# The 48 short logits products of a routed part in two portions of 24, and the scatters of one-unit blocks released one by one

## The chip, the cores and the metric

The kernel runs on one core of one Trainium2 chip. The metric is the device time of one execution in microseconds, as the median of several runs; lower is better. One further execution was taken by the hardware profiler, and all views below come from it.

## The reference

The input is x, 8 sequences of 3584 tokens of 192 floats. Stage one is a causal depthwise convolution of 7 taps, whose taps are a softmax over 7 weights for each of 8 heads (24 channels a head). Stage two is a mixture of experts with one expert for each token:

```
logits = x @ w_gate                       # 8 experts
local  = sigmoid(x @ w_local)
e[s]   = argmax(logits[s])   if s == 0 or local[s] < 0.5   else e[s-1]
out[s] = softmax(logits[s])[e] * (relu(x[s] @ w1[e]) @ w2[e])     # 192 -> 1024 -> 192
```

All of it is float32. There are 28672 tokens in all.

## The kernel before, in words

The tokens are worked on in 16 **parts** of 1792 tokens. For each part VectorE and ScalarE compute the convolution (`conv`, lines L378 and L388), and then the part is **routed** (`route`): its logits are computed, the expert of each token is found by a long chain of small VectorE operations, and each token's row is scattered into a table of slots in DRAM (`put`, L777), sorted by expert. Parts 0 and 1 are handled by a special path at the start (`wide`, `wide_route`); the other 14 go through `route`.

A **unit** is 128 slots of one expert. A **block** is one unit (n = 1) or two units (n = 2) of one expert. The 142 blocks are the main work. The first 35 blocks or so have one unit, the bulk after about 267 us has two, and the last 20 have one again. For block i, SyncE's queue loads the expert's weights (`load_w`, L906, 1.5 MB, four buffers) and the rows (`load_rows`, L913) three blocks ahead. TensorE then does, in this order:

- `hidden` of block i (L963): products with w1 in two groups, `two` = 0 and 1. After each group ScalarE applies the ReLU (L968). The PSUM tiles come from `hps_p`, which has four buffers.
- `turn` of block i + 1 (L360): transposes of the next rows into the PSUM tile of `xps_p`, which has one buffer; ScalarE copies them out (L947, L949).
- `output` of block i (L980): products with w2 into `yps_p`. ScalarE and VectorE scale and add the two halves (L988, L992), and GpSimd scatters the rows to the output (L996).

Float32 products show as two weight loads and two matmuls each in the trace. "A pair" below is one LDWEIGHTS with its MATMUL, so 48 products are 96 pairs. One-unit blocks hold 48 pairs of L963, 8 of L360 and 32 of L980; two-unit blocks hold 48, 16 and 64.

Between these steps, `step(time)` is called three times a block: after `turn`, inside `output` (`step(1.2)`, after L988 is issued) and after `output`. It takes VectorE operations from two generators, `route` and `conv`, until their estimated times add up to `time`. When `route` yields "hop", the rest of this `step` goes to `conv`, and `route` goes on in the next `step`. The order of all instructions is fixed when the program is built; nothing is decided at run time.

The logits of a part (`logits`) are where the change lies. VectorE transposes the rows into the tile z (L572). Then TensorE runs 48 short products (L582): 64 rows by 32 columns of weights, 128 columns of data, in two halves of the rows and four groups of columns, so eight of them can be in the array at a time. They accumulate over six steps b in two PSUM tiles of `hps_p`. ScalarE copies the results out (L587), and VectorE transposes and sorts them (L590, L598). So each of the 14 parts has one unbroken run of 96 short pairs at L582, put into TensorE's order where `route` happens to reach it: in ten parts between L360 and L980 of a two-unit block, in one between L360 and L980 of a one-unit block, and in three after L980 (in one-unit blocks).

Two scatters of rows (`put`) go with each block that has any to do; they are held back until a ReLU is done. `put(relu)` adds that wait to the scatter on GpSimd's queue. In two-unit blocks one is released by the ReLUs of `two` = 0 and one by those of `two` = 1; in one-unit blocks both are released by those of `two` = 1.

Of the kernel before, what the change touches and what calls it, by code (L numbers as in the profile page):

```python
# [8 lines left out]
F32 = mybir.dt.float32  # L9
# [8 lines left out]
P = 128  # L18
# [19 lines left out]
BT = 2 * UT  # L38
KT = BT // P
# [24 lines left out]
Q = 32  # L64
DQ = D // Q
TQ = (NT + 3) // 4
# [15 lines left out]
def kernel(  # L82
# [10 lines left out]
    nc = tc.nc  # L93
# [11 lines left out]
    xps_p = ctx.enter_context(tc.tile_pool(name="xps_p", bufs=1, space=PSUM))  # L105
    hps_p = ctx.enter_context(tc.tile_pool(name="hps_p", bufs=4, space=PSUM))
# [77 lines left out]
    wgb, wgq = wg[:, :3, :], wg[:, 3:, :]  # L184
# [5 lines left out]
    def z_tile():  # L190
        return yt.tile([P, 3 * NH * TB + NB * DR], F32, name="z")
# [119 lines left out]
    rows = cst.tile([Q, 2, Q], F32, name="rows")  # L311
# [42 lines left out]
    def halves():  # L354
        return [(half, slice(half * DR, (half + 1) * DR)) for half in range(2)]
# [210 lines left out]
    def logits(g, y_sb):  # L566

        nc.gpsimd.tensor_copy(y_sb[:, :, Y0 + D:IX], y_sb[:, :, Y0 + P:Y0 + D])  # L568
        z = z_tile()[:, :NT * D].rearrange("p (t d) -> p t d", d=D)
        for t in range(0, NT, TQ):  # L570
            u = min(t + TQ, NT)
            nc.vector.transpose(z[:, t:u, :], y_sb[:, t:u, Y0:Y0 + D])  # L572
            yield 0.2 * (u - t)
        yield "hop"


        lps = [hps_p.tile([P, TQ * Q], F32, name="hps") for half in range(2)]
        begin = [min(TQ * j, NT - TQ) for j in range(4)]
        for b in range(DQ):
            for j in range(4):  # L580
                for half, rows in halves():
                    nc.tensor.matmul(lps[half][Q * j:Q * j + Q, :], lhsT=wgq[rows, b, :],  # L582
                                     rhs=z[rows, begin[j]:begin[j] + TQ, b * Q:(b + 1) * Q],
                                     start=(b == 0), stop=(b == DQ - 1))
        ls = sm.tile([P, 2, TQ * Q], F32, name="ls", bufs=1)
        for half in range(2):
            nc.scalar.copy(ls[:, half, :], lps[half])  # L587
        yield "hop"
        lq = sm.tile([P, 2 * TQ, Q], F32, name="lq", bufs=1)
        nc.vector.transpose(lq.rearrange("p t e -> p (t e)"), ls.rearrange("p h x -> p (h x)"))  # L590
        yield 0.4
        lt = sm.tile([P, NT + 2, E + 1], F32, name="lt")
        for r in range(4):
            for j in range(4):
                t, u = TQ * j, min(TQ * (j + 1), NT)
                at = r // 2 * TQ + t - begin[j]
                e0 = r % 2 * (E + 1)
                nc.vector.tensor_copy(lt[Q * r:Q * r + Q, t:u, :],  # L598
                                      lq[Q * j:Q * j + Q, at:at + u - t, e0:e0 + E + 1])
                yield 0.12  # L600
        return lt
# [168 lines left out]
    def put(behind=None):  # L770


        if not to_put:
            return
        g, rows, to = to_put.pop(0)
        nc.gpsimd.nop()
        ins = nc.gpsimd.indirect_dma_start(  # L777
            out=slots[:, :], in_=rows, in_offset=None,
            out_offset=bass.IndirectOffsetOnAxis(ap=to, axis=0)).ins
        if behind is not None:  # L780
            tc.add_manual_dep(ins, behind.ins.name, SYNC, reason="scatters apart")
        if puts:
            tc.declare_no_dep(ins, group="puts", reason="slots of their own")
        if g:
            tc.declare_no_dep(ins, group="gets", reason="those slots were full before")
        puts.append((g, ins))
        tc.add_to_no_dep_group("puts", ins)
        tc.add_to_no_dep_group(f"puts{g}", ins)
# [163 lines left out]
    def hidden(n, wb, xT, shares=(1, 1)):  # L952
        hT = hp.tile([P, FK, BT], F32, name="hT")
        w = slice(0, n * P)


        for two in range(2):
            hps = [hps_p.tile([P, 2, BT], F32, name="hps") for half in range(2)]
            for d in range(KD):
                for j in range(2):  # L960
                    f0 = (d * 4 + two * 2 + j) * P
                    for half, rows in halves():
                        nc.tensor.matmul(hps[half][:, j, w], lhsT=wb[rows, f0:f0 + P],  # L963
                                         rhs=xT[rows, d, w], start=(d == 0 and j == 0),
                                         stop=(d == KD - 1), skip_group_check=True)
            for half in range(2):
                m = half * 4 + two * 2
                relu = nc.scalar.activation(hT[:, m:m + 2, w], hps[half][:, :, w], Act.Relu)  # L968
            for _ in range(shares[two] if n == KT else (0, sum(shares))[two]):
                put(relu)  # L970
        return hT

    def output(n, wb, xg, hT):

        yps = [yps_p.tile([P, 512], F32, name="yps") for half in range(2)]
        for m4 in ([0, 1, 4, 5], [2, 3, 6, 7]):
            for k in range(n):
                for m in m4:
                    for half, rows in halves():
                        nc.tensor.matmul(yps[half][:, k * D:(k + 1) * D],  # L980
                                         lhsT=hT[rows, m, k * P:(k + 1) * P],
                                         rhs=wb[rows, WA + m * D:WA + (m + 1) * D],
                                         start=(m == 0 and k == 0), stop=(m == FK - 1),
                                         skip_group_check=True)
        o_sb = op.tile([P, KT, D], F32, name="o_sb")
        y = [[yps[half][:, k * D:(k + 1) * D] for half in range(2)] for k in range(n)]
        for k in range(n):
            nc.scalar.activation(o_sb[:, k, :], y[k][0], Act.Copy, scale=xg[:, k, 0:1])  # L988

        step(1.2)  # L990
        for k in range(n):
            nc.vector.scalar_tensor_tensor(o_sb[:, k, :], y[k][1], xg[:, k, 0:1], o_sb[:, k, :],  # L992
                                           Alu.mult, Alu.add)

            nc.gpsimd.nop()
            sent = nc.gpsimd.indirect_dma_start(  # L996
                out=out, in_=o_sb[:, k, :], in_offset=None,
                out_offset=bass.IndirectOffsetOnAxis(ap=xg.bitcast(I32)[:, k, IX:], axis=0),
                bounds_check=N - 1, oob_is_err=False)
            tc.declare_no_dep(sent.ins, group="sent", reason="each token has one slot")  # L1000
            tc.add_to_no_dep_group("sent", sent.ins)
# [1 line left out]

    LEAD = 2
    LATE = 3
    st = {"block": 0, "conv": 1, "cgen": None, "route": 1, "rgen": None, "routed": 1}

    def start_conv():
        g = st["conv"] + 1
# [14 lines left out]
    def start_route():  # L1024
        done = st["conv"] - (st["cgen"] is not None)
        if st["rgen"] is None and st["route"] < done:
            st["route"] += 1
            st["rgen"] = route(st["route"])

    def route_op():  # L1030
        c = next(st["rgen"], None)
        if c is None:
            st["rgen"] = None
            st["routed"] = st["route"]
        return c

    def step(time):

        start_route()
        start_conv()  # L1040
        go = st["rgen"] is not None
        while time > 0:
            c = route_op() if go else conv_op()
            if c is None:
                if not go:
                    break
                go = False
            elif c == "hop":
                go = False
            elif c == "placed":  # L1050
                pass
            else:
                time -= c
# [76 lines left out]
    xT, _ = turn(blocks[0][1], xgs[0])  # L1130
# [8 lines left out]
    for i, (_, n, _, _) in enumerate(blocks):  # L1139
        st["block"] = i  # L1140
        ensure(i)
        weights(i + AHEAD)
        if i == LATE:
            x_in[3] = load_x(3)
        hT = hidden(n, wbs[i], xT, (1, 1) if i else (0, 0))
        if i + 1 < len(blocks):
            xT, copied = turn(blocks[i + 1][1], xgs[i + 1])
            if len(to_put) > NT // 2 and n == KT:
                put(copied)
        step(2.1 if n == 1 else 4.2)  # L1150
        output(n, wbs.pop(i), xgs.pop(i), hT)
        step(1.3 if n == 1 else 3.0)

    kind, _, at, group = spare[0]
    any_left = nc.values_load(tabi[kind, group][at:at + 1, 0:1], min_val=0, max_val=DUMMY,  # L1155
                              skip_runtime_bounds_check_because="an entry of the table")
    with tc.If(any_left < DUMMY):
        for block in spare:
            blocks.append(block)
            i = len(blocks) - 1  # L1160
            n = block[1]
            xg = load_rows(i)
            wb = load_w(i)
            xT, _ = turn(n, xg)
# [68 lines left out]
```

## Time and profile before

| what | value |
|---|---|
| median of 7 runs | 1337.73 us (1335.65 to 1341.74) |
| the profiled execution | 1335.88 us, span 1334.2 us |
| TensorE matmuls, weight loads busy | 98%, 95% of the span |
| VectorE, ScalarE, GpSimd busy | 58%, 44%, 37% |
| granted TensorE clock, mean | 0.998 |
| DMA busy, 60 to 335 us / 335 to 935 us | 0.91 / 0.67 |
| L980, L963, L360, L582 matmuls busy | 643.7, 636.4, 62.0, 26.4 us |

A busy share of TensorE says only that some matmul was in flight. Matmuls overlap, so what a run of them costs is read from when the next line begins, and an interval in which too few were in flight can hide in a busy time. The table of waits names what ended an engine's idle time; "issue" stands for idle time in which the profile shows nothing that the engine waited for.

### The profile page before, as it was taken

Reading aid. Unit: us, or ns where it says so; the run is one execution under the profiler, and the core shown is the slowest. Engines: PE = TensorE matmul, PEld = TensorE weight load, DVE = VectorE, ACT = ScalarE, POOL = GpSimd, SP = SyncE. Lnnn points to the kernel's source line nnn. Section 1 sums busy time; section 2 is a strip of 40 time slices with the busy share of each in tenths; the row PEclk is TensorE's granted clock in tenths of the full one; section 3 lists DMA queues with packets and bytes.
Section 4 is the critical chain, followed back from the end, with each engine's and each line's share of the span. In section 5 each row is a group of like instructions: output and inputs, shape, how many; then the busy total and the mean of one; then the engine's idle time right before and its main releaser. Section 6 shows DMA issues by size and latency. Waiting matters only on the chain. (4 is left out here: it accounts for less than half of the span.)

```text
span 1334.2 us, 41246 instructions
## 1 busy us (share of the span) xinstructions
PE 1309.5 (98%) x16682; PEld 1267.8 (95%) x16682; DVE 779.1 (58%) x2434; ACT 583.1 (44%) x1431; POOL 492.5 (37%) x538
## 2 busy tenths in 40 slices
PE   8799999999999999999999999999999999999997
PEld 7799999999999999999999999999999999999997
DVE  6879897877878787878777878786610000000000
ACT  5345554544444444444444444444343333334443
POOL 4445343534243434343434343434344211211111
PEclk9999999999999999999999999999999999999999
DMA  5899999967575757575757575756566555556893
GB/s 187 279 354 390 388 371 357 385 244 276 197 281 197 294 202 291 199 282 202 289 195 287 202 293 205 289 206 230 204 235 223 201 185 188 194 195 230 320 332 126
DMA packets 67297, 340.35 MB, mean 255 GB/s; under 512 B 12576, under 2 KB 23191, under 8 KB 47650
## 3 DMA queue, kind: packets, MB, share of 16 engines
q1 hardware_dynamic: 44784, 284.88, 59.4%
q0 software_dynamic: 22320, 52.82, 10.5%
q8 instruction: 133, 2.18, 0.6%
q14 instruction: 58, 0.48, 0.1%
q10 hardware_dynamic: 2, 0.00, 0.0%
HBM read 284.73 MB, written 53.41 MB: 253 GB/s over the span
## 5 line engine op out<-in xcount | busy, mean ns | idle before, releaser
L980 PE MATMUL yps<-wb,hT 64*128 64x192 f32 x7328 | 643.7, 326 | 5.5 <-DVE o_sb L992 2.8
L963 PE MATMUL hps<-xT,wb 64*128 64x256 f32 (+1 forms) x6816 | 636.4, 336 | 3.8 <-issue 2.4
L980 PEld LDWEIGHTS yps<-wb,hT 64*128 64x128 f32 x7328 | 605.5, 188 | 11.6 <-issue 6.6
L963 PEld LDWEIGHTS hps<-xT,wb 64*128 64x128 f32 x6816 | 592.0, 187 | 25.0 <-issue 4.3
L996 POOL DMA_INDIRECT out_dram<-o_sb,xg x229 | 232.2, 1014 | 602.4 <-DVE o_sb L992 540.7
L968 ACT ACTIVATE hT<-hps 128x512 f32<-128x512 f32 (+1 forms) x568 | 261.5, 512 | 371.8 <-PE hps L963 284.3
L388 DVE SCALAR_TENSOR_TENSOR y_sb<-x_sb,c,y_sb 128x336 f32<-128x336 f32 x672 | 377.2, 571 | 18.6 <-issue 0.5
L992 DVE SCALAR_TENSOR_TENSOR o_sb<-yps,xg,o_sb 128x192 f32<-128x192 f32 x229 | 87.5, 414 | 472.9 <-ACT o_sb L988 459.2
L777 POOL DMA_INDIRECT slots<-y_sb,posi x228 | 228.0, 1000 | 210.6 <-ACT hT L968 90.5
L988 ACT ACTIVATE o_sb<-yps,xg 128x192 f32<-128x192 f32 x229 | 86.8, 418 | 323.9 <-PE yps L980 321.4
L949 ACT COPY xT<-xps 64x256 f32<-64x256 f32 (+1 forms) x284 | 92.2, 325 | 6.9
L947 ACT COPY xT<-xps 128x512 f32<-128x512 f32 (+1 forms) x142 | 72.5, 511 | 4.5 <-issue 1.9
L360 PEld LDWEIGHTS xps<-ident,xg 64*128 64x128 f32 x916 | 61.9, 138 | 5.2 <-issue 0.4
L378 ACT ACTIVATE y_sb<-x_sb,c 128x336 f32<-128x336 f32 x112 | 63.7, 581 | 1.0
L360 PE MATMUL xps<-ident,xg 64*128 64x64 f32 x916 | 62.0, 221 | 0.0
L572 DVE STREAM_TRANSPOSE z<-y_sb 128x768 f32<-128x768 f32 (+1 forms) x56 | 45.4, 852 | 0.4
L598 DVE COPY lt<-lq 32x36 f32<-32x36 f32 x224 | 40.8, 182 | 3.5
L582 PE MATMUL hps<-z,wg 64*32 64x128 f32 x1344 | 26.4, 273 | 2.7 <-issue 2.7
L582 PEld LDWEIGHTS hps<-z,wg 64*32 64x32 f32 x1344 | 19.9, 105 | 6.9 <-issue 6.1
L590 DVE STREAM_TRANSPOSE lq<-ls 128x256 f32<-128x256 f32 x14 | 6.2, 440 | 13.5 <-ACT ls L587 13.5
L568 POOL COPY y_sb<-y_sb 128x896 f32<-128x896 f32 x14 | 13.3, 952 | 0.0
L556 PE MATMUL yps<-y_sb 112*128 112x194 f32 x64 | 11.5, 331 | 1.8 <-DVE y_sb L550 1.8
(240 smaller groups left out, 384.0 us busy)
## 6 DMA issues: line engine op xcount, KB each, us to landing
wb<-in_w_dram SPq DMA_DIRECT2D x138, 1536.0 KB
x_sb<-in_x_dram SPq DMA_DIRECT2D x14, 1920.0 KB
xg<-slots SPq DMA_DIRECT2D x87, 259.0 KB
xg<-slots SPq DMA_DIRECT2D x53, 129.5 KB
wb<-in_w_dram SPq DMA_DIRECT2D x12, 512.0 KB
out_dram<-o_sb,xg POOLq DMA_INDIRECT x229
slots<-y_sb,posi POOLq DMA_INDIRECT x228
x_sb<-in_xb_dram SPq DMA_DIRECT2D x4, 768.0 KB
```

Of the source, the lines that this page charges most:

```text
L360: nc.tensor.transpose(to, src[rows], identity=ident[rows, rows])
L378: nc.scalar.activation(cols(h), chans(h, 0), Act.Copy, scale=c[:, h, 0:1])
L388: nc.vector.scalar_tensor_tensor(cols(h), chans(h, k), c[:, h, k:k + 1], cols(h), Alu.mult, Alu.add)
L777: ins = nc.gpsimd.indirect_dma_start(out=slots[:, :], in_=rows, in_offset=None, out_offset=bass.IndirectOffsetOnAxis(ap=to, axis=0)).ins
L947: nc.scalar.copy(first, by)
L949: copied = nc.scalar.copy(to[rows, :, 2], at[(DR, 0)[half]:(P, DR)[half], :, 0])
L963: nc.tensor.matmul(hps[half][:, j, w], lhsT=wb[rows, f0:f0 + P], rhs=xT[rows, d, w], start=(d == 0 and j == 0), stop=(d == KD - 1), skip_g ...
L968: relu = nc.scalar.activation(hT[:, m:m + 2, w], hps[half][:, :, w], Act.Relu)
L980: nc.tensor.matmul(yps[half][:, k * D:(k + 1) * D], lhsT=hT[rows, m, k * P:(k + 1) * P], rhs=wb[rows, WA + m * D:WA + (m + 1) * D], start= ...
L988: nc.scalar.activation(o_sb[:, k, :], y[k][0], Act.Copy, scale=xg[:, k, 0:1])
L992: nc.vector.scalar_tensor_tensor(o_sb[:, k, :], y[k][1], xg[:, k, 0:1], o_sb[:, k, :], Alu.mult, Alu.add)
L996: sent = nc.gpsimd.indirect_dma_start(out=out, in_=o_sb[:, k, :], in_offset=None, out_offset=bass.IndirectOffsetOnAxis(ap=xg.bitcast(I32)[ ...
```

## The change

The 48 short products of a part are cut at b = 3 into two portions of 24 (48 pairs each), and longer products run between the two.

- Where `route` reaches the products in the `step` between `turn` and `output` (`st["ahead"]`), the first portion is put there, and `route` then hops. The second portion and ScalarE's copies come in the next `step`, inside `output`: between L980 of this block and L963 of the next. The PSUM tiles are from `hps_p` as before, and are held longer. Eleven parts go this way.
- Where `route` reaches them elsewhere, the first portion is put there, into the tile of `xps_p`, and the second one is left as a function in `st["amid"]`. `hidden` of the next block calls it after its first group (`two` = 0): between 12 products of L963 and the 12 that follow. Three parts go this way, the first, second and fourth of the 14.
- The rule that in one-unit blocks both scatters wait for the second pair of ReLUs is gone; they are released one by one, as in two-unit blocks.

No product, copy or scatter is added or taken away. In the order of instructions the portions are the only thing that moves on TensorE. On VectorE the transposes and copies after the logits (L590, L598) come a few operations of `conv` later, behind the L992 of the block. On SyncE's queue one load of a part's input moves behind one load of rows and one of weights, and on GpSimd's queue two scatters move ahead of one copy (L568).

```diff
-        lps = [hps_p.tile([P, TQ * Q], F32, name="hps") for half in range(2)]
+        if st["ahead"]:
+            lps = [hps_p.tile([P, 2 * BT], F32, name="hps") for half in range(2)]
+        else:
+            both = xps_p.tile([P, 2, 512], F32, name="xps")
+            lps = [both[:, half, :] for half in range(2)]
+        lps = [a[:, :TQ * Q] for a in lps]
         begin = [min(TQ * j, NT - TQ) for j in range(4)]
-        for b in range(DQ):
-            for j in range(4):
-                for half, rows in halves():
-                    nc.tensor.matmul(lps[half][Q * j:Q * j + Q, :], lhsT=wgq[rows, b, :],
-                                     rhs=z[rows, begin[j]:begin[j] + TQ, b * Q:(b + 1) * Q],
-                                     start=(b == 0), stop=(b == DQ - 1))
+        def products(bs):
+            for b in bs:
+                for j in range(4):
+                    for half, rows in halves():
+                        nc.tensor.matmul(lps[half][Q * j:Q * j + Q, :], lhsT=wgq[rows, b, :],
+                                         rhs=z[rows, begin[j]:begin[j] + TQ, b * Q:(b + 1) * Q],
+                                         start=(b == 0), stop=(b == DQ - 1))
         ls = sm.tile([P, 2, TQ * Q], F32, name="ls", bufs=1)
-        for half in range(2):
-            nc.scalar.copy(ls[:, half, :], lps[half])
-        yield "hop"
+        def others():
+            products(range(DQ // 2, DQ))
+            for half in range(2):
+                nc.scalar.copy(ls[:, half, :], lps[half])
+        products(range(DQ // 2))
+        if st["ahead"]:
+            yield "hop"
+            others()
+            yield "hop"
+        else:
+            st["amid"] = others
+            while st["amid"]:
+                yield "hop"
...
-            for _ in range(shares[two] if n == KT else (0, sum(shares))[two]):
+            for _ in range(shares[two]):
                 put(relu)
+            if st["amid"]:
+                st["amid"]()
+                st["amid"] = None
...
+        st["ahead"] = True
         step(2.1 if n == 1 else 4.2)
+        st["ahead"] = False
```

## The prediction

> **What bounds the kernel now.** I read the page first, then TensorE's table of waits, then the timeline of TensorE around the logits of each part. The page says that TensorE's matmuls are in flight for 98% of the span at a granted clock of 0.998, and of L582, the line that is changed:
>
> ```profile
> L582 PE MATMUL hps<-z,wg 64*32 64x128 f32 x1344 | 26.4, 273 | 2.7 <-issue 2.7
> ```
>
> Its 1344 matmuls are 14 parts by 96 pairs, and they cover 26.4 us. The change leaves their number alone, so only their neighbourhood can pay. The waits of the weight loads, first from 60 to 275 us (one-unit blocks), then from 275 to 1330 us:
>
> ```profile
> PEld hps L582 <- issue: 6.1, 14, 0.6
> PEld hps L963 <- issue: 4.3, 13, 0.5
> ```
>
> ```profile
> PEld yps L980 <- issue: 4.8, 16, 0.9
> ```
>
> No wait for a DMA stands among them: weights and rows are there in time. What TensorE waits for is "issue", that is, its own instructions. The timeline of TensorE shows a clean case, the last part, in a two-unit block, and the block after it:
>
> ```profile
> 927.74 5.35 PE L963 MATMUL hps<-xT,wb 64*128 64x256 f32 x48
> 932.92 0.41 PE L360 MATMUL xps<-ident,xg 64*128 64x64 f32 x8
> 933.26 1.59 PE L582 MATMUL hps<-z,wg 64*32 64x128 f32 x96
> 934.79 5.47 PE L980 MATMUL yps<-wb,hT 64*128 64x192 f32 x64
> 940.09 5.35 PE L963 MATMUL hps<-xT,wb 64*128 64x256 f32 x48
> ...
> 950.77 4.49 PE L963 MATMUL hps<-xT,wb 64*128 64x256 f32 x40
> ```
>
> From the first L963 to the next, the block with logits takes 940.09 - 927.74 = 12.35 us, the one without 950.77 - 940.09 = 10.68: a clean stage costs 1.67 us. The 96 pairs start 13.9 ns apart ((1.59 - 0.27) / 95, where 0.27 is one matmul), together 1.32 us. The other 0.35 us are entering and leaving: the short products start only when the matmul before has nearly ended, and the same holds when they leave.
>
> Two of the early parts look different (the third of the 14, then the first):
>
> ```profile
> 205.91 1.29 PE L582 MATMUL hps<-z,wg 64*32 64x128 f32 x56
> 207.42 0.42 PE L582 MATMUL hps<-z,wg 64*32 64x128 f32 x5 [0.22 <-issue]
> ...
> 209.69 0.67 PE L582 MATMUL hps<-z,wg 64*32 64x128 f32 x23 [0.33 <-issue]
> 210.29 2.87 PE L980 MATMUL yps<-wb,hT 64*128 64x192 f32 x32
> ```
>
> ```profile
> 88.83 1.23 PE L582 MATMUL hps<-z,wg 64*32 64x128 f32 x38
> 90.36 0.42 PE L582 MATMUL hps<-z,wg 64*32 64x128 f32 x4 [0.31 <-issue]
> ...
> 91.80 1.08 PE L582 MATMUL hps<-z,wg 64*32 64x128 f32 x52 [0.35 <-issue]
> 92.81 1.39 PE L963 MATMUL hps<-xT,wb 64*128 64x128 f32 x20
> ```
>
> Some pairs run at full speed, then TensorE gets a handful of instructions every 0.75 us, then the rest come in a burst. I read this as a store of ready instructions that the short pairs (14 ns each, against 83 to 107 ns for the long ones in two-unit blocks) empty faster than it is filled. The supply is slower here, in the stretch where DMA is 0.91 busy (0.67 later).
>
> **The pool that can be won.** Stage times by the timeline, from the first L582 to the next line: 3.98, 2.20, 4.38, 2.33 us for the first four parts, 1.53 for a clean one. The four lose 2.45 + 0.67 + 2.85 + 0.80 = 6.8 us. The other ten run through L582 without a gap, but some of their L980 stall afterwards: their blocks take 13.06, 12.53, 12.66, 12.96, 12.62, 13.45, 12.53, 12.48, 12.35, 12.35 us, 3.5 us over ten clean ones. Blocks without logits of the same stretch lie within 1.4 us of 10.68 in sum, so the 3.5 belong to the stages.
>
> **The change part by part.**
>
> *More entries and exits (certain, on the path).* Each part gets one more run of short pairs. Between L980 and L963 the timeline's starts are 0.25 us into the run and 0.20 out of it, and the direct turn from L980 to L963 that this replaces is 0.15: 0.30 us net. For the three portions amid L963 no such entry is in the trace; after L360 (matmul 221 ns) it takes 0.15, after L980 (326 ns) 0.25, so after L963 (273 or 376 ns) 0.20 to 0.30, less its own step of 0.10 to 0.20, plus 0.20 out: 0.30 again. Bounds 0.20 and 0.45. 14 x 0.30 = +4.2 us (2.8 to 6.3).
>
> *Two-unit blocks (ten of the parts).* Half the run empties half as much of the store, and 64 pairs of L980 at 83 ns (5.3 us) lie between the portions. At its emptiest the store gave 96 short pairs and 26 long ones (part at 668.9 us, then a stall of 0.65 us). With 48 short pairs fewer it lasts 48 x 83 ns = 4 us longer, beyond that stall. I take -3.3 of the 3.5 us (-1.5 to -3.5).
>
> *Third part (one-unit block, "ahead").* It runs 56 pairs before its first real stall, so 48 pass untouched. Then 32 pairs of L980 need 2.7 us, in which the supply gave only 17 pairs before, and some 8 are left: about 7 pairs short, one stall of 0.6. -2.85 + 0.6 = -2.2 us (0 to -2.85).
>
> *First, second and fourth part (portion two amid L963).* Portion one stands exactly where the whole run stood, and their stalls come after 33 to 44, 28 and 33 pairs, all inside the first 48. They stay. What is saved is at most a tail, -0.3 in all; what may be added is a stall before portion two, because 24 pairs of L963 at 58 ns do not refill the store: +0.6 once. Together +0.3 us (-2.5 to +1.8, the upper end being a stall of 0.6 in each of the three).
>
> *Copies and tiles.* ScalarE's two L587 (0.27 us each) move behind L988 or between the ReLUs. The tile of `xps_p` is wanted by `turn` only after 24 more pairs of L963 (1.4 us), which hides them; without that cover 0.5 us in each of three blocks. The `hps_p` tiles held longer are wanted by `two` = 1 of the next block, 1.4 to 2.6 us later. 0. VectorE's L590 and L598 come later by two to four `conv` operations of 0.57 us; L992 moves ahead of them, and scatters of the part keep their place in GpSimd's order. VectorE's longest waits are for ScalarE, not the reverse. 0.
>
> *SyncE.* One load of x (1.9 MB) goes behind one load of rows and one of weights, one block (5.5 us) later; it is needed after half a part of convolution (24 operations of 0.57 us = 14 us). 0.
>
> *Earlier release of scatters.* GpSimd in the block at 86 us:
>
> ```profile
> 87.59 0.96 POOL L777 DMA_INDIRECT slots<-y_sb,posi  x1 [1.66 <-issue]
> 88.86 0.94 POOL L777 DMA_INDIRECT slots<-y_sb,posi  x1 [0.31 <-issue]
> 90.11 0.99 POOL L996 DMA_INDIRECT out_dram<-o_sb,xg  x1 [0.30 <-DVE o_sb L992]
> ```
>
> The first of the three would go some 1.4 us earlier, in idle time. Behind it on GpSimd are the second scatter and L996; L996 waits for L992, which ended at 89.80, as did the second scatter, so it gains nearly nothing. TensorE waits for none of these. 0 (-1 to +1, since a DMA moved against the short pairs could change their supply).
>
> *Sum.* +4.2 - 3.3 - 2.2 + 0.3 = -1.0 us. The profiled execution of 1335.88 (span 1334.2 and 1.7 around it) becomes 1334.9; it lay 1.85 below the median shown, so the median becomes 1336.7. That is 0.07% less: no change. I count 0.2% (2.7 us) as about what a measurement of this kernel can tell.
>
> A rule weighed. The row: in the clean parts 96 short pairs, 192 instructions, run without a gap, and the early parts stop after 28 to 56 pairs. The Trainium skill, "TensorE: Matmul & The Clock Gate", the table at its head, gives TensorE a queue 64 deep. That would be 32 pairs, near the three early stops, and it speaks against this change, for a portion of 48 pairs overruns it too: by the rule alone every portion would stall, 28 x 0.6 us, +16.8 + 4.2 - 10.3 = some +11 us (an estimate). The clean parts contradict that, so my sum goes by the rows.
>
> **The rivals.** *Stalls go almost wholly* (faster). If a stall is set off by the length of a run and not by how full the store was, all portions pass: -6.8 - 3.5 + 4.2 = -6.1, 1331.6 us. For it: after one stall, parts two and four run 63 to 68 pairs in one burst. Against: their first stall comes by pair 33. Chance 0.29 with all that gains over 2.7 us.
>
> *The supply sets the pace in one-unit blocks* (slower). Then a portion amid L963 or after L980 finds the store empty, and the stalls only move. For it: L963 shows issue stalls there without any logits (4.3 us). Price: +4.2, the early parts win nothing and two or three new stalls of 0.6 come, the later parts win only 1.5: +4.2 + 1.5 - 1.5 = +4.2, 1341.9 us. It decides if portion two of the early parts begins with fewer than 48 pairs in store. Chance 0.27 with all that loses over 2.7 us.
>
> *The split does nothing and the scatters decide*: the portions' gain and loss cancel, and the release shifts times by up to 1 us: within the 0.2%.
>
> **How the numbers follow.** The middle case has 0.44 (the last rival included): faster 0.29, same 0.44, slower 0.27. The range runs to the middle of each neighbouring case and somewhat beyond: 1332.3 to 1341.3 us.
>
> **What would show it.** Right: two-unit blocks with logits all at 10.68 + 1.67 + 0.30 = 12.65 us; the third part without repeated gaps in its first portion; the first, second and fourth with a gap still near pair 30; two more starts of 0.2 to 0.25 us for each part. Wrong: gaps at L963 or L980 after second portions in the early blocks, waits of L360 for the `xps_p` tile, or early blocks that got shorter by 2 us each.

## The result, and the profile after

| | before | changed |
|---|---|---|
| median on the chip of the first measurement | 1336.81 us (1333.37 to 1341.74, 34 runs) | 1339.48 us (1339.04 to 1342.71, 13 runs) |
| ratio, 95% interval | | 1.0027 [1.0018, 1.0036] |
| the profiled execution, and its span | 1335.88 us, 1334.2 us | 1339.83 us, 1338.1 us |
| same on two chips of the experiments (3 and 15), medians | 1320.62 us (25 runs), 1319.99 us (25 runs) | 1322.33 us, 1322.3 us |
| ratios there | | 1.0014 [1.0004, 1.0024], 1.0015 [1.0006, 1.0025] |

The changed kernel is a little slower: by 0.27% by the ratio and 0.20% by the medians, about as much as the prediction thought could be told at all. All experiments ran on three chips (numbers 3, 9 and 15 on record) on which the very same kernel takes some 17 us less. I call these the 1320-us chips, and that of the first measurement the 1337-us chip. The record has no number for the latter, so that the 17 us belong to the chip itself, and not to its condition at that time, is the likely reading and not shown. Nearly everything below hangs on that difference.

In the changed kernel the lines are: hidden products L985 (before L963), logits L591 (L582), output products L1005 (L980), ReLU L990 (L968), scaling L1013 (L988), scatter of slots L799 (L777), scatter of outputs L1021 (L996).

**The two-unit blocks.** TensorE's timeline at the last part, 1337-us chip, the columns being start, length, engine, line, operation and count:

```profile
931.51 5.35 PE L985 MATMUL hps<-xT,wb 64*128 64x256 f32 x48
936.69 0.41 PE L360 MATMUL xps<-ident,xg 64*128 64x64 f32 x8
937.03 0.94 PE L591 MATMUL hps<-z,wg 64*32 64x128 f32 x48
937.90 5.47 PE L1005 MATMUL yps<-wb,hT 64*128 64x192 f32 x64
943.30 0.94 PE L591 MATMUL hps<-z,wg 64*32 64x128 f32 x48
944.17 5.45 PE L985 MATMUL hps<-xT,wb 64*128 64x256 f32 x48
...
954.95 1.25 PE L985 MATMUL hps<-xT,wb 64*128 64x256 f32 x10
```

The block takes 944.17 - 931.51 = 12.66 us (12.65 was forecast). The one after it takes 954.95 - 944.17 = 10.78 instead of 10.68, and its hidden products 5.45 instead of 5.35: 0.10 us that the forecast did not have. Eight of the ten blocks are at 12.66, two at 12.78 and 12.83; no portion there has a gap.

**The parts in one-unit blocks.** The third part, which had paused again and again:

```profile
209.86 0.89 PE L591 MATMUL hps<-z,wg 64*32 64x128 f32 x18
211.03 0.80 PE L591 MATMUL hps<-z,wg 64*32 64x128 f32 x30 [0.29 <-issue]
211.76 2.87 PE L1005 MATMUL yps<-wb,hT 64*128 64x192 f32 x32
214.56 0.94 PE L591 MATMUL hps<-z,wg 64*32 64x128 f32 x48
```

One gap after 18 pairs, the rest unbroken. The first part has one of 0.15 us after pair 29 of its first portion, the second part one of 0.31 us after pair 42 of its second portion, the fourth none; nothing like the former trickle is left.

**The waits, 60 to 275 us.** TensorE's weight loads by what they waited for (total us, times, longest):

```profile
PEld yps L1005 <- ACT hT L990: 14.0, 21, 1.0
PEld hps L985 <- issue: 2.8, 11, 0.4
...
PEld xps L591 <- issue: 1.8, 5, 0.6
PEld hps L591 <- issue: 1.1, 3, 0.6
```

The issue waits at the logits fell from 6.1 to 2.9 us. But output products now wait 21 times for the ReLUs, nearly always in ordinary one-unit blocks without logits. In the same table of before this line was

```profile
PEld yps L980 <- ACT hT L968: 0.7, 2, 0.4
```

Here is one such wait, the block that starts at 182.89, on three engines (TensorE, ScalarE, GpSimd):

```profile
182.89 2.84 PE L985 MATMUL hps<-xT,wb 64*128 64x128 f32 x48
...
185.68 1.52 PE L1005 MATMUL yps<-wb,hT 64*128 64x192 f32 x16
187.48 1.57 PE L1005 MATMUL yps<-wb,hT 64*128 64x192 f32 x16 [0.27 <-ACT hT L990]
188.88 0.50 PE L985 MATMUL hps<-xT,wb 64*128 64x128 f32 x6
```

```profile
184.48 0.66 ACT L990 ACTIVATE hT<-hps 128x256 f32<-128x256 f32 x2 [0.51 <-ACT y_sb L378]
187.04 0.66 ACT L990 ACTIVATE hT<-hps 128x256 f32<-128x256 f32 x2 [1.90 <-PE xps L360]
```

```profile
184.23 1.06 POOL L1021 DMA_INDIRECT out_dram<-o_sb,xg  x1 [1.30 <-DVE o_sb L1017]
185.60 0.97 POOL L799 DMA_INDIRECT slots<-y_sb,posi  x1 [0.30 <-issue]
```

The second group of L985 is done at 185.73 (182.89 + 2.84). Its ReLUs start at 187.04, 1.3 us later, though ScalarE is idle (the row names L360, which TensorE had done by then as well; the tile that the ReLUs read is L985's). Ahead of both lies the start of the scatter that the change released earlier, at 185.60, 1.44 us before the ReLUs. The output products that read these ReLUs start late, and the block takes 188.88 - 182.89 = 5.99 us instead of 5.45. In the kernel before, a block at nearly the same time shows the same delay in a small dose: a scatter starts at 182.95, TensorE's second group ends at 183.56 by the same timeline, and the ReLUs start 1.39 us after the scatter did.

```profile
184.34 0.66 ACT L968 ACTIVATE hT<-hps 128x256 f32<-128x256 f32 x2 [0.93 <-PE xps L360]
```

```profile
182.95 1.06 POOL L996 DMA_INDIRECT out_dram<-o_sb,xg  x1 [0.92 <-DVE o_sb L992]
```

There the ReLUs were 0.8 us late, and the block lost 0.07 us. So there is a slack of some 0.74 us, and the change pushed the delay beyond it.

**The ledger.** Times from the first hidden product of a block to the next, summed over blocks, in the two profiled executions of the 1337-us chip, beside the terms of the forecast:

| stretch | before, us | changed, us | difference | forecast |
|---|---|---|---|---|
| the four parts in one-unit blocks and the block behind (8 blocks) | 65.54 | 61.49 | -4.05 | 1.2 - 2.2 + 0.3 = -0.7 |
| ten two-unit blocks with a part | 126.99 | 126.90 | -0.09 | 3.0 - 3.3 = -0.3 |
| the ten blocks behind them | 107.00 | 107.83 | +0.83 | 0 |
| the other 26 one-unit blocks up to 267 us (269 us) | 146.85 | 156.04 | +9.18 | 0 |
| to the end of the first two blocks | 65.37 | 63.60 | -1.76 | 0 |

The first four lines add to +5.9. The last line is no part of the change that I can name: on the 1320-us chips the same point lies between 63.2 and 65.2 us in the fifteen profiled executions, whichever variant runs. The executions as a whole differ by +3.95 us, the medians by +2.67.

Of the 26 blocks of the fourth line, four have no scatter to release (they start at 159.6, 165.0, 221.0 and 226.4 us in the changed kernel). These four take 5.45 us each; the other 22 take 5.84 to 6.46. That ties the longer blocks to the scatters and not to the split, which no block of this line contains.

**Signals after a scatter.** The trace holds the moment at which a semaphore, the signal from one engine to another, moves. I compared it with the end of the matmul that moves it, and sorted by whether the matmul ended within 1.4 us after GpSimd started an indirect DMA. "Late" is more than 0.3 us; the usual delay is 0.01 us. TensorE's signals:

| execution | 92 to 260 us: late, within 1.4 us | late, otherwise | 330 to 900 us: late, within 1.4 us | otherwise |
|---|---|---|---|---|
| before, 1337-us chip | 88 of 127 | 1 of 75 | 57 of 236 | 0 of 143 |
| changed, 1337-us chip | 81 of 147 | 0 of 48 | 33 of 249 | 0 of 129 |
| before, a 1320-us chip (f2) | 1 of 128 | 0 of 81 | 7 of 267 | 0 of 111 |
| changed, a 1320-us chip (f1) | 1 of 122 | 0 of 85 | 0 of 257 | 0 of 125 |

On the 1337-us chip more than half of TensorE's signals sent in the 1.4 us after such a start come late in the one-unit blocks. In the changed kernel the late ones arrive 1.49 us (median) after the scatter's start, as if held until then. On the other chip this hardly happens. ScalarE's starts agree. I took the second ReLUs of the one-unit blocks from 63 to 270 us for which ScalarE had been idle. Where the products ended within 1.4 us of a scatter's start, the ReLUs began over 0.3 us late in 10 of 24 cases before and 23 of 29 after the change on the 1337-us chip, in 0 of 22 and 0 of 27 on the other; where they did not, never.

For the signals of ScalarE and VectorE the trace shows no such thing. On the 1337-us chip it lacks the moments of 240 of ScalarE's 1428 signals and 295 of VectorE's 1764 in the kernel before (53 of TensorE's 1088; in f2 it lacks 2, 8 and none), and where one is missing, the next one of that engine would pass for a late one. The receiver can be looked at instead. Here, 0.49 us after the scatter that started at 88.86 us, ScalarE ends at 89.35 and VectorE starts 0.03 us later, though the trace has no signal of ScalarE in the next 3.8 us:

```profile
88.93 0.42 ACT L988 ACTIVATE o_sb<-yps,xg 128x192 f32<-128x192 f32 x1 [1.29 <-PE yps L980]
```

```profile
89.38 0.42 DVE L992 SCALAR_TENSOR_TENSOR o_sb<-yps,xg,o_sb 128x192 f32<-128x192 f32 x1 [2.60 <-PE yps L980]
```

In the two profiled executions of that chip I found six such cases with VectorE idle; it started 0.03 us after ScalarE's end in four, 0.18 and 0.35 us after it in two.

The Trainium skill, "Perfetto Trace Analysis", Per-engine timelines, lists the spreading of a semaphore update as a step behind a matmul's recorded end and gives no time for it. The trace has 0.01 us for it mostly, and 1.3 us in these blocks.

### The profile page after: what moved, and what is told of

Same layout as the page of the kernel before. It is cut to its first block, busy times and chain, and to the rows that moved or that the text cites. A ratio compares the mean times of both kernels' runs of the same rounds, so it can differ in the third digit from the quotient of the medians.

```text
span 1338.1 us, 41275 instructions
## 1 busy us (share of the span) xinstructions
PE 1311.1 (98%) x16682; PEld 1242.6 (93%) x16682; DVE 781.3 (58%) x2434; ACT 582.9 (44%) x1431; POOL 491.0 (37%) x538
## 5 line engine op out<-in xcount | busy, mean ns | idle before, releaser
L1005 PE MATMUL yps<-wb,hT 64*128 64x192 f32 x7328 | 637.2, 326 | 12.6 <-ACT hT L990 8.4
L985 PE MATMUL hps<-xT,wb 64*128 64x256 f32 (+1 forms) x6816 | 627.4, 336 | 0.7 <-issue 0.7
L1005 PEld LDWEIGHTS yps<-wb,hT 64*128 64x128 f32 x7328 | 595.1, 187 | 22.8 <-ACT hT L990 15.3
L985 PEld LDWEIGHTS hps<-xT,wb 64*128 64x128 f32 x6816 | 564.6, 187 | 41.0 <-issue 2.8
L1021 POOL DMA_INDIRECT out_dram<-o_sb,xg x229 | 232.1, 1014 | 598.7 <-DVE o_sb L1017 534.0
L990 ACT ACTIVATE hT<-hps 128x512 f32<-128x512 f32 (+1 forms) x568 | 261.7, 512 | 403.1 <-PE hps L985 253.5
L799 POOL DMA_INDIRECT slots<-y_sb,posi x228 | 226.7, 994 | 219.8 <-ACT hT L990 84.3
L1013 ACT ACTIVATE o_sb<-yps,xg 128x192 f32<-128x192 f32 x229 | 86.8, 418 | 308.8 <-PE yps L1005 303.1
L360 PEld LDWEIGHTS xps<-ident,xg 64*128 64x128 f32 x916 | 52.2, 139 | 7.4
L360 PE MATMUL xps<-ident,xg 64*128 64x64 f32 x916 | 53.3, 221 | 0.0
L591 PE MATMUL hps<-z,wg 64*32 64x128 f32 x1056 | 21.4, 275 | 0.3 <-issue 0.3
L591 PEld LDWEIGHTS hps<-z,wg 64*32 64x32 f32 x1056 | 14.9, 105 | 4.1 <-issue 3.3
L556 PEld LDWEIGHTS yps<-y_sb 112*128 112x128 f32 x64 | 11.9, 212 | 2.6 <-DVE y_sb L550 2.0
L568 POOL COPY y_sb<-y_sb 128x896 f32<-128x896 f32 x14 | 13.3, 951 | 0.0
```

The lines of the kernel that those rows point to most:

```text
L360: nc.tensor.transpose(to, src[rows], identity=ident[rows, rows])
L799: ins = nc.gpsimd.indirect_dma_start(out=slots[:, :], in_=rows, in_offset=None, out_offset=bass.IndirectOffsetOnAxis(ap=to, axis=0)).ins
L1005: nc.tensor.matmul(yps[half][:, k * D:(k + 1) * D], lhsT=hT[rows, m, k * P:(k + 1) * P], rhs=wb[rows, WA + m * D:WA + (m + 1) * D], start= ...
L1021: sent = nc.gpsimd.indirect_dma_start(out=out, in_=o_sb[:, k, :], in_offset=None, out_offset=bass.IndirectOffsetOnAxis(ap=xg.bitcast(I32)[ ...
```

## The experiments

Five theories stood at one time or another. R: the earlier release of the scatters is the cost. S: the split of the products is. C: what the release costs depends on the chip. D: only both together cost. H, formed last: signals are held after a scatter's start, on the 1337-us chip and not on the others. L (the late ReLUs alone make the block longer) and W (they do not) concern one link of it.

### The two halves of the change

Split only: the changed kernel, with both scatters again behind the second pair of ReLUs in one-unit blocks.

```diff
-            for _ in range(shares[two]):
+            for _ in range(shares[two] if n == KT else (0, sum(shares))[two]):
```

Release only: the kernel before, with the opposite edit alone. The changed kernel (f1, h3) and the kernel before (f2) ran beside them.

> The changed kernel with one part undone: in one-unit blocks both scatters are again released by the second pair of ReLUs. Theory R (the early release of the first scatter is the cost: it delays the second pair of ReLUs by 1.3 us in some 22 one-unit blocks, and TensorE waits 0.55 us in each): L1005 no longer waits for hT in the one-unit blocks, these take 5.45 to 5.6 us, and the time is 4 to 10 us below the changed kernel, 1330 to 1335 us. Theory S (the split is the cost: one more entry and exit of short products for each part, 0.3 us each, and a wait of the next block for ScalarE): the time stays within 1.5 us of the changed kernel, 1338 to 1341 us.

> The kernel before with only the release changed: one scatter for each pair of ReLUs in one-unit blocks, the 48 short products in one run. Theory R: the second pair of ReLUs starts 1.3 us late in the one-unit blocks with scatters, which take about 6.0 us; the time is 5 to 10 us above the kernel before, 1342 to 1347 us. Theory S: no change, 1336 to 1338 us.

> The changed kernel itself, beside its parts on one chip. The first four experiments ran on a chip on which the kernel before takes 1320 us instead of 1337, and there the release alone changed nothing. Theory C (the cost of the early release depends on the chip: only where signals and instructions arrive late in the one-unit blocks does it delay the second ReLUs): on a chip of about 1320 us the changed kernel has no waits of L1005 for hT in one-unit blocks and costs only what the split costs, 0.1 to 0.2% over the kernel before; on a chip of about 1337 us it costs 0.2 to 0.4%, with some 20 waits of L1005 for hT. Theory D (split and release together delay the ReLUs, each alone does not): the waits are there on either chip.

> The kernel before, for a profile on the same chip. Theory C: on a chip of about 1320 us its one-unit blocks lack the issue gaps (6.8 us at L582 and about 6 us in blocks without logits in the first profile) and are 10 us shorter in sum; on a chip of about 1337 us they are there. Theory D makes no difference here.

> The kernel before with only the release changed, again. Theory C: on a chip of about 1320 us within 0.1% of the kernel before; on a chip of about 1337 us 0.3 to 0.8% slower, with the second ReLUs of one-unit blocks late by 1.3 us. Theory D: within 0.1% on either.

> The changed kernel with both scatters of one-unit blocks behind the second ReLUs, again. Theory C: on a chip of about 1320 us 0.1 to 0.2% slower than the kernel before, as in the first run; on a chip of about 1337 us 0.2 to 0.6% faster. Theory D: 0.1 to 0.2% slower on the first; on the second it says only that the waits of L1005 are gone.

> The kernel before with only the earlier release of the first scatter in one-unit blocks. Theory H (a signal between engines that is sent within 1.4 us after GpSimd starts an indirect DMA is held until about 1.45 us after that start on the chip of 1337 us, and not on the one of 1320 us): where the kernel before takes about 1337 us this one is 9 to 13 us slower than it, less up to 3 us for shorter stalls in the one-unit parts (ratio 1.005 to 1.009), with some 20 waits of TensorE's output products for hT; where it takes about 1320 us, ratio 0.999 to 1.0005 and none of these waits. Rival S (the split alone is the cost, on either chip): within 0.1% of before on both.

> The changed kernel with both scatters again behind the second pair of ReLUs. Theory H: where the kernel before takes about 1337 us, the split alone takes out part of the stalls between the short products there (7 to 8 us of them in all) and pays 0.3 to 0.4 us for each of 14 second portions: ratio 0.995 to 1.000; where it takes about 1320 us there are no such stalls to take and the ratio is 1.001 to 1.002. Rival S: 1.001 to 1.003 on both.

> The changed kernel itself, beside its two halves. Theory H: where the kernel before takes about 1337 us, the sum of the two halves, 1.002 to 1.0035; where it takes about 1320 us, the split's cost alone, 1.001 to 1.002, with no signal of TensorE, ScalarE or VectorE over 0.3 us late. Rival S: 1.001 to 1.003 on both, and the release-only kernel equal to before.

The times named in the first four expectations (e1 to e4) are those of the 1337-us chip. None was met, all four came out at 1319 to 1322 us, and only their ratios can be read.

| 1320-us chips | ratio to before, 95% interval |
|---|---|
| split only (e1, f4, h2) | 1.0014 [1.0005, 1.0023], 1.0019 [1.001, 1.0029], 1.0016 [1.0006, 1.0026] |
| release only (e2, f3, h1) | 0.9993 [0.9984, 1.0002], 1.0003 [0.9993, 1.0013], 0.9999 [0.999, 1.0009] |
| both (f1, h3) | 1.0014 [1.0004, 1.0024], 1.0015 [1.0006, 1.0025] |

f2, the kernel before itself, took 1319.36 us. On these chips the split is the whole cost and the release costs nothing: R falls there, S holds, D falls. The head of the changed kernel's table of waits (f1), 60 to 275 us:

```profile
PEld hps L985 <- issue: 2.3, 8, 0.9
PEld xps L591 <- issue: 0.8, 3, 0.3
PEld hps L591 <- issue: 0.2, 1, 0.2
```

The line with hT is gone, and so are the issue waits that the split was to shorten. A block of f1 with the released scatter, ScalarE and GpSimd:

```profile
187.18 0.66 ACT L990 ACTIVATE hT<-hps 128x256 f32<-128x256 f32 x2 [0.62 <-PE hps L985]
```

```profile
185.92 1.06 POOL L1021 DMA_INDIRECT out_dram<-o_sb,xg  x1 [1.59 <-DVE o_sb L1017]
187.29 0.97 POOL L799 DMA_INDIRECT slots<-y_sb,posi  x1 [0.30 <-issue]
```

TensorE's second group ends here about 1.25 us after a scatter's start (L1021), inside the 1.4 us, and the ReLUs start at once. The one-unit blocks without logits between 63 and 253 us take at most 5.52 us each in f1, h3, e2 and h1, but for one of 6.74 and 6.88 us in e2 and h1 that the kernel before has too (6.68 in f2). The released scatter itself mostly starts later here, 2.7 to 4.0 us into a block instead of 2.7 to 3.3, so often behind the end of the second group at 2.87; what speaks against held signals are the 27 second groups that ended within 1.4 us of some scatter's start and had their ReLUs on time. So on these chips the traces have no held signals, and the release has nothing to cost, as C and H say. That is half of a proof: no experiment reached the 1337-us chip, and the release alone was never timed there.

### The first scatter earlier still

The changed kernel, where the first scatter of a one-unit block waits for no ReLU.

```diff
-                put(relu)
+                put(relu if n == KT or two else None)
```

> The changed kernel, but in one-unit blocks the first scatter waits for no ReLU; GpSimd issues it as soon as it is through with the scatter to the output before it, at about the same moment as now. If what matters is the moment (a scatter issued while the second group of products ends keeps TensorE's signal from ScalarE until 1.45 us after the scatter's start), the second ReLUs stay late by about 1.3 us and the time stays at 1337 to 1341 us. If the scatter's wait for the first ReLUs matters, the ReLUs are on time and the time falls to 1330 to 1335 us.

1.0018 [1.0007, 1.0029], as the changed kernel itself within the intervals. But the edit hardly moved the scatter: by the traces it starts 2.6 to 4.1 us into these blocks in f1 and in e3, apart from one block (1.41 instead of 2.63). And with no held signals here, the run cannot tell its two cases apart. It shows only that the wait for the ReLU is not what sets the scatter's start.

### Late ReLUs made on purpose

The kernel before, on a 1320-us chip, with copies on ScalarE that delay the second ReLUs of the 29 one-unit blocks with scatters: five copies (g1) or three (g2).

```diff
+            if n == 1 and two == 1 and to_put:
+                for _ in range(5):
+                    nc.scalar.copy(hT[:, 2:4, w], hT[:, 0:2, w])
             for half in range(2):
```

> The kernel before, with five copies on ScalarE (128x256, computing nothing that is used: they write the half of hT that the second pair of ReLUs then overwrites) ahead of the second pair of ReLUs in the one-unit blocks that have scatters to put (29 blocks). By the row of the same kernel a 128x256 copy takes 0.38 us, so the second pair starts at about 2.25 + 5 x 0.38 = 4.15 us into the block instead of 2.87, which is where the changed kernel's stood on the chip of the first measurement. Theory L (on that chip it was the late start of the second ReLUs, by about 1.3 us, that made the block longer, whatever made it late): those blocks take 6.0 us instead of 5.45, TensorE's second half of the output products waits for hT, and the kernel is 12 to 17 us slower (29 x 0.55). Rival W (the block was longer for another reason, such as the scatters' transfers, and the late ReLUs only went with it): blocks stay at 5.45 us and the kernel within 2 us.

> As the one before with three copies in place of five: the second pair of ReLUs starts at about 2.25 + 3 x 0.38 = 3.4 us into the block, 0.5 us late. Theory L with a slack of about 0.75 us between the second ReLUs and the output products that read them: blocks stay at 5.45 us, no wait for hT, the kernel within 0.2% of before. If there is no such slack: 29 x 0.5, up to 14 us slower.

g1: 1337.17 us, ratio 1.0132 [1.0118, 1.0147], 17.2 us, just above the 12 to 17 of theory L. Its waits (60 to 275 us), ScalarE's copies, and TensorE in one block:

```profile
PEld yps L983 <- ACT hT L971: 18.9, 26, 1.0
```

```profile
123.35 2.15 ACT L968 COPY hT<-hT 128x256 f32<-128x256 f32 x5
125.54 0.66 ACT L971 ACTIVATE hT<-hps 128x256 f32<-128x256 f32 x2
```

```profile
124.01 1.52 PE L983 MATMUL yps<-wb,hT 64*128 64x192 f32 x16
125.97 1.57 PE L983 MATMUL yps<-wb,hT 64*128 64x192 f32 x16 [0.44 <-ACT hT L971]
```

It is the picture of the 1337-us chip, the output products cut in two by a wait for hT. A copy took 0.41 us where I had 0.38, so the ReLUs start at 4.32 us into the block, and the block takes 6.16 us. g2: ReLUs at 3.45 us into the block, most blocks at 5.45, ratio 1.0006 [0.9997, 1.0015], no wait for hT. One rule fits both: a block takes 5.45 us plus what the second ReLUs start later than 3.61 us into it (4.32 - 0.71). Over the 26 other one-unit blocks it gives 16.1 us for g1, where 16.1 was measured; that is no test, since the rule is drawn from g1. In g2 two blocks have their ReLUs later than 3.61 us, at 3.74 and 3.71; the rule says 5.58 and 5.55 us, and they take 5.58 and 5.62. Put on the changed kernel of the 1337-us chip, with the starts its trace shows, it gives 12.9 of its 14.3 us over 26 times 5.45; on the kernel before, 1.3 of 5.1 (the rest there are issue waits and late first ReLUs). So late second ReLUs account for 11.6 us more than before, and the other waits for 2.4 less: together the +9.2 of the ledger. L holds, W falls: late second ReLUs explain the longer blocks, whatever makes them late.

### Where the split's cost lies

Splits only in the four parts of one-unit blocks, both scatters late (e4), only in the ten two-unit parts with the release as changed (g4), and the whole change with ScalarE's two copies ahead of the scaling (g3).

```diff
         if st["ahead"]:
-            yield "hop"
+            if st["n"] > 1:                # g4; in e4: == 1
+                yield "hop"
             others()
...
         if st["ahead"]:
-            yield "hop"
-            others()
-            yield "hop"
+            st["second"] = others          # g3
+            while st["second"]:
+                yield "hop"
...
+        if st["second"]:                   # g3, in output
+            st["second"]()
+            st["second"] = None
         for k in range(n):
             nc.scalar.activation(o_sb[:, k, :], y[k][0], Act.Copy, scale=xg[:, k, 0:1])
```

> Both scatters of one-unit blocks released by the second pair of ReLUs, and the products split only where the block has one unit (four of the 14 parts); the ten parts in two-unit blocks run their 48 products in one run, as before the change. In the changed kernel the ten two-unit blocks with a part take 20.1 us over ten without, as much as before (20.2), and each block after them is 0.1 us longer, so the split gains nothing there: by theory R this kernel is 0 to 2 us faster than the one with the split everywhere and both scatters late, 1329 to 1334 us. By theory S it stays at 1337 us or more.

> The changed kernel with the products of a part in two portions only in the ten two-unit blocks; the four parts in one-unit blocks run theirs as before. Theory S by blocks: ten times (12.66 - 12.44) + 0.10 = 3.2 us, less one or two of the rare stalls of before of 0.2 to 0.7 us: 2.2 to 3.2 us slower than before, 1.0017 to 1.0025; the four other parts cost nothing measurable. Rival: the cost lies in the one-unit blocks' parts (1.2 to 1.5 us) and this one stands at 1.0005 to 1.0012.

> The changed kernel with one thing different: in the two-unit blocks the second portion and its two copies out of PSUM are issued ahead of the scaling of o_sb on ScalarE instead of behind it. Theory: the 0.1 us that TensorE's next hidden products wait for these copies is gone; the block after each two-unit block with a part is 10.68 us again instead of 10.78, ten times, 1.0 us in all, so the kernel stands at about 1.0007 to 1.0012 times before instead of 1.0014 to 1.0019. Rival: the copies then hold up the scaling and the scatters of the output, and with them the next block's output products; nothing gained, or up to 2 us lost.

e4: 1.0012 [0.9996, 1.0027], undecided. g4: 1.0022 [1.0013, 1.003], so the ten parts alone cost as much as the whole change. By blocks: split parts take 12.66 and the block behind 10.78 in g4, f1 and g3 alike; unsplit ones 12.44 and 10.68, apart from a few with a stall of 0.1 to 1.3 us. That is 0.22 + 0.10 = 0.32 us for one more run of short pairs, 3.2 us over ten. In the seven unsplit executions the stalls give back 1.0 to 1.9 us of it. g4 and e4 together come to more than the whole change; the intervals are wide enough for that, and I make nothing of it.

g3: 1.0023 [1.0014, 1.0031], no gain. In the changed kernel the table of waits names a releaser there (f1, the whole span):

```profile
PEld hps L985 <- issue: 3.6, 9, 1.4
...
PEld hps L985 <- ACT o_sb L1013: 2.0, 10, 0.2
```

L985 waits ten times, 2.0 us in all, for ScalarE's L1013, from which I had concluded that the copies queued behind L1013 cost TensorE this time. With the copies moved (g3), that wait is gone, and the blocks still take 10.78:

```profile
PEld hps L985 <- issue: 5.6, 19, 1.4
```

The 0.10 us belongs to leaving a short run: in f1 and g3 alike the first two matmuls of L985 behind it take 0.48 us instead of 0.38, the third starts 0.10 us later, and the rest keep their pace. The releaser named was the one that happened to be last. My theory fell.

## Why the prediction was right or wrong

The range held the time; the likeliest case, no change, did not come (1.0027 [1.0018, 1.0036]). That the time stayed inside the range is luck: 9.2 us that no term foresaw in blocks without logits met 3.4 us more gain than forecast in the early parts and 1.8 us at the start that no term names. Step by step:

- **Entries and exits, 14 x 0.30.** Right within a tenth: 0.32 us by the two-unit blocks of the 1320-us chips. The part that shows in the next block (0.10) was missing from the picture, not much from the sum. On the 1337-us chip the clean pairs ran closer before (12.35 us instead of 12.44), so there it is 0.31 + 0.10.
- **Two-unit blocks, -3.3.** Held: 12.66 against 12.65, stalls gone but for two of 0.1 to 0.2 us. With the 0.10 behind, the ten parts came to +0.7 us instead of -0.3.
- **Third part, -2.2, and parts one, two and four, +0.3.** With the entries this forecast -0.7; measured -4.05, in spite of some 1.1 us of held signals in blocks 15 and 34 (counted from 0; they hold the second and the fourth part). The third part, with its entry, gave -1.5 where -1.9 was forecast; its one stall came in the first portion, which was to pass, and the second portion passed. The term that was mis-sized is the first, second and fourth part: with entries +1.2 was forecast, and -2.55 measured (-1.76, -0.21, -0.58). "They stay" was wrong, the stalls mostly went. Why is open. That shorter portions stall less is one reading; but in the second and the fourth part TensorE had also just waited 0.31 and 0.16 us for late ReLUs ahead of the first portion, and of the four first portions only those two passed without a gap. The rule weighed, 64 places and a stall in every portion, finds no support: three of the 28 portions have a gap.
- **Copies and tiles, 0.** Right, by g3, although a table of waits says otherwise.
- **Earlier release of scatters, 0 (-1 to +1).** This is the step that failed, on the 1337-us chip: +9.2 us in blocks without any logits, by the traces, since the release alone was not timed there. Its reasoning, "TensorE waits for none of these", looked for who waits for the scatter's data. What mattered is who sends a signal while the scatter starts: TensorE's second group does, 0.1 us later, and its ReLUs started 1.3 us late, with a slack of 0.74. Both bounds were drawn from short pairs and their supply, and the profile of before already showed the cause: 88 of TensorE's 127 signals within 1.4 us of a scatter's start were late there. ScalarE's ReLUs starting late beside idle time is where it could be read.
- **The rivals.** "The supply sets the pace" ended on the right side for a wrong reason: waits for instructions got fewer. "Stalls go almost wholly" had the stalls nearly right and the outcome wrong, since the release took it back. "The scatters decide" was put at 1 us; they decided, at nine times that.
- **What I could not know from one profile.** The pool of stalls (10.3 us by my count) and the held signals are both there on the one chip and almost absent on the others. On the 1320-us chips the forecast's entries alone, less 1 to 2 us of stalls, come to 2 to 3 us, where 1.7 to 2.3 were measured.

What is shown by experiments: the price of the split in the two-unit blocks and where it lies, the release's price on the 1320-us chips (none), and that ReLUs as late as those of the 1337-us chip make blocks as long as those there. What is read from traces alone: that TensorE's signals are late there, almost only after a scatter's start, and that the blocks with a released scatter are the longer ones. What stays open: the time of the release alone and of the split alone on that chip, what holds the signals, and why the early stalls went.

## What to carry to other kernels

When a DMA issue is moved, look also at which signals of other engines are sent in the time after its new start (a microsecond and a half on the 1337-us chip), and what slack their receivers have; a transfer nobody waits for can still lengthen the critical path. A longer run of short products is cheaper than two short ones unless it really stalls: each more run cost 0.32 us here. And a stall seen in one profile may belong to the chip, or to its condition at the time, rather than to the kernel, so a change that lives off it should be timed on a second one.

## What the runs showed of the hardware

- The same kernel took 1336.81 us in the first measurement and about 1320 us on three chips later, at a granted clock of 0.998 and 0.995 in the profiled executions. Of the difference between two profiled executions (16.5 us), 11.9 lie in the first 33 one-unit blocks after the start (201.6 against 189.7 us) and 2.8 in blocks 35 to 101.
- After GpSimd started an indirect DMA, TensorE's signals were often late on the 1337-us chip (81 of 147 in the one-unit blocks of the changed kernel), until about 1.49 us after that start, and on a 1320-us chip not (1 of 122). For ScalarE and VectorE no such delay is shown.
- The issue waits at bursts of short products differ as much: 6.1 us at L582 in the one-unit blocks on the 1337-us chip, 0.5 us in the same table of a 1320-us chip (f2).
- The first two 64x256 products behind a run of short ones take 0.48 us instead of 0.38.
- A releaser named by a table of waits, ten times with the same 0.2 us, was not the cause.
